# Loading and normalising the first tile of k and q in chunks ahead of the rest of k, with GpSimd normalising the rest

## The chip, the cores and the metric

The kernel runs on one core of a Trainium2 chip. The core has five engines with a queue each, which go through their instructions in order and wait for each other by semaphores: TensorE (PE in the profile; its weight loads are PEld), VectorE (DVE), ScalarE (ACT), GpSimd (POOL) and SyncE (SP, here a queue that issues loads and stores). The metric is the device time of one execution in microseconds (us).

## The reference

```python
def _attn_ref(q, k, v, g_q, g_k):                 # q, k, v: (8, 12, 448, 64) float32
    def rmsnorm(x, g):
        return x / np.sqrt(np.mean(x * x, axis=-1, keepdims=True) + 1e-06) * g
    q_n, k_n = (rmsnorm(q, g_q), rmsnorm(k, g_k))
    scores = 1.0 / np.sqrt(64) * np.matmul(q_n, k_n.transpose(0, 1, 3, 2))
    attn = np.exp(scores - np.max(scores, axis=-1, keepdims=True))
    attn = attn / (np.sum(attn, axis=-1, keepdims=True) + 1e-09)
    return np.matmul(attn, v)
...
x = attn_out.transpose(0, 2, 1, 3).reshape(8 * 448, 12 * 64)
h = x @ w_in                                      # (768, 2048)
return np.maximum(0.01 * h, h) @ w_out            # (2048, 768)
```

So: attention with normalised q and k, and behind it a layer of two matrices with a leaky ReLU between them.

## The kernel before, in words

The attention is cut into 24 units (`u`, three for each of the 8 batches) of four heads. In SBUF a unit's q and k lie as tiles `rq` and `rk` of 128 partitions, with 2 halves (`a`) of 7 groups of rows (`t`) of 64 elements each. One unit goes through these steps:

- `load(u)` issues the loads of q and k on SP's queue. Three buffers of each are in turn, so that the loads of units 1 and 2 could start at once. `hold` puts a small copy on POOL in the way, which writes one element of unit 1's tiles and reads one of a tile of unit 0: the loads of unit 1 wait for that copy, and so for the data that it reads.
- `prep_sq` (ACT) or `prep_sqp` (POOL) squares, `prep_ssq` sums each row's squares on VectorE, `prep_rinv` turns the sums into 1/sqrt on ACT with a Ln and an Exp, `prep_norm` multiplies the row by it on VectorE and writes it as float16 to `n16`.
- The normalised tiles are transposed, in the first units by TensorE (`tr`, `prep_tr`; the bank is then copied to `qkT` by `vcopy` on VectorE or `acopy` on ACT). For q the copy multiplies by the gains: `gcol` is a column that holds 0.125 times g_q times g_k. It is made from two loaded rows: `gdup` (VectorE, line 869) and a small float32 matmul (line 870) that turns the row into a column in the bank `gps`, which is copied to `gcol`.
- `qk` makes the scores of k's tile `t` against all of q in a pair of PSUM banks. For a unit's first tile `shift_max`, `shift_mm` find a maximum over the scores (VectorE, a matmul, VectorE), from which the exponent's shift `eb` is made. `ex` takes the exponential of a score pair on ACT into `et`.
- `zsum`, `pv` sum and weigh with v on TensorE, and later steps divide. Three units make a batch, and then the two matrices follow (`moe1`, lines 432 and 440, then lines 478 and 542).

K0 is k's first tile (0 to 1), K1 the other six (1 to 7); CA and CB are the groups 0 to 4 and 4 to 7.

The order of the work in the opening is written out by hand, line by line, for all engines (lines 858 to 1075); from unit 3 on a plan in a loop mixes attention with the matrices. `warm(n, bank)` is `n` matmuls of a constant that nothing reads (line 847), which keep TensorE running. `gate(u)` is a small copy on POOL that reads the normalised k: what stands behind it in POOL's queue (loads of v and of the weights, squares) waits until VectorE has normalised unit u. In the opening before, q and k of unit 0 are loaded by one transfer each, both on SP; the squares of both stand on ACT, all normalising on VectorE, and the small matmul of the gains stands between 32 and 48 filling matmuls. The lines that decide on the order:

```python
warm(32, wbank)
...                        # gdup, and the matmul of the gains
warm(48, wbank)
prep_sq(0, CA, (0,))
prep_sq(0, CB, (0,))
prep_sq(0, ALL, (1,))
...                        # sums, Ln and Exp for q, then for k
prep_norm(0, CA, (0,))
prep_norm(0, CB, (0,))
prep_norm(0, K0, (1,))
prep_norm(0, K1, (1,))
```

Of the kernel before, what the change touches and what calls it, by code (L numbers as in the profile page):

```python
# [8 lines left out]
FP32 = mybir.dt.float32  # L9
FP16 = mybir.dt.float16  # L10
AF = mybir.ActivationFunctionType
ALU = mybir.AluOpType
AXL = mybir.AxisListType
# [5 lines left out]
def kernel(  # L19
# [11 lines left out]
    nc = tc.nc  # L31

    B, H, S, D = q.shape
    QH = 4
    NS = 7
    P = 128
# [9 lines left out]
    raws = ctx.enter_context(tc.tile_pool(name="raws", bufs=3))  # L46
    prep_p = ctx.enter_context(tc.tile_pool(name="prep", bufs=2))
    small = ctx.enter_context(tc.tile_pool(name="small", bufs=2))
# [12 lines left out]
    def mine(i):  # L61
        return shared or i < 4
# [7 lines left out]
    def aux(bank=None):  # L70
        can = [i for i in free if mine(i) and bank in (None, i)]
        if shared:
            can = [i for i in can[:-1] if i ^ 1 not in free] or can
        free.remove(can[0])
        return single[can[0]]

    def slot():
        if shared:
            can = [i for i in free if i ^ 1 in free]
            last = {i // 2: n for n, i in enumerate(free) if i in can}  # L80
        else:
            last = {i // 2: n for n, i in enumerate(free) if i >= 4 and i ^ 1 in free}
        x = min(last, key=lambda i: last[i])
        for i in (2 * x, 2 * x + 1):
            free.remove(i)
        return double[x]

    def drop(tile_):
        for i in range(8):
            if tile_ is single[i]:  # L90
                assert i not in free
                free.append(i)
                return
        x = [i for i in range(4) if tile_ is double[i]][0]
        assert 2 * x not in free and 2 * x + 1 not in free
        free.extend((2 * x, 2 * x + 1))
# [11 lines left out]
    eps_t = cst.tile([P, 1], FP32)  # L108
# [6 lines left out]
    gcol = cst.tile([P, 1], FP32)  # L115
# [22 lines left out]
    raw = {}  # L138
    st = {}

    def rows(x, u):
        b, g = divmod(u, NQ)
        return x[b, QH * g:QH * g + QH].rearrange("(a r) (p t) d -> (r p) a (t d)", r=2, t=NS)

    def load(u, engines=None, hold=None):
        raw[u] = [raws.tile([P, 2, NS, D], FP32, tag=name, name=name) for name in ("rq", "rk")]
        st[u] = {}
        if hold is not None:
            for t in raw[u]:
                nc.gpsimd.tensor_copy(t[:, 1, NS - 1, D - 1:D], hold[:, 1, NS - 1, D - 1:D])  # L150
        for t, src, eng in zip(raw[u], (q, k), engines or (nc.sync, nc.sync)):
            eng.dma_start(t.rearrange("p a t d -> p a (t d)"), rows(src, u))

    def load_v(u):
        nc.gpsimd.dma_start(vts[u % NV].rearrange("p a t d -> p a (t d)"), rows(v, u))

    ALL = (0, NS)
# [4 lines left out]
        rinv=([P, 2, 2, NS], FP32, 2),  # L162
        n16=([P, 2, NS, 2, D], FP16, 1), qkT=([P, 2, NS, P], FP16, 3))

    def buf(u, name):
        if name not in st[u]:
            shape, dtype, bufs = SHAPES[name]
            st[u][name] = prep_p.tile(shape, dtype, tag=name[:2] if bufs == 3 and name != "qkT" else name, bufs=bufs, name=name)
        return st[u][name]

    BOTH = (0, 1)

    def prep_sq(u, c=ALL, tis=BOTH):
        for ti in tis:
            nc.scalar.activation(buf(u, f"sq{ti}")[:, :, c[0]:c[1]], raw[u][ti][:, :, c[0]:c[1]], AF.Square)  # L175

    def prep_sqp(u, tis=BOTH):
        for ti in tis:
            nc.gpsimd.tensor_tensor(buf(u, f"sq{ti}"), raw[u][ti], raw[u][ti], op=ALU.mult)
# [4 lines left out]
    def prep_ssq(u, c=ALL, tis=BOTH):  # L184
        for ti in tis:
            nc.vector.tensor_reduce(buf(u, "ssq")[:, ti, :, c[0]:c[1]], buf(u, f"sq{ti}")[:, :, c[0]:c[1]],  # L186
                                    axis=AXL.X, op=ALU.add)

    def prep_rinv(u, tis=BOTH):
        x = slice(tis[0], tis[-1] + 1)  # L190
        nc.scalar.activation(buf(u, "uu")[:, x], buf(u, "ssq")[:, x], AF.Ln, bias=eps_t, scale=1.0 / D)
        nc.scalar.activation(buf(u, "rinv")[:, x], buf(u, "uu")[:, x], AF.Exp, bias=0.0, scale=-0.5)  # L192

    def prep_norm(u, c=ALL, tis=BOTH):
        n = c[1] - c[0]
        for ti in tis:
            src = raw[u][ti]
            nc.vector.tensor_tensor(  # L198
                buf(u, "n16")[:, ti, c[0]:c[1]].rearrange("p s a d -> p a s d"), src[:, :, c[0]:c[1]],
                buf(u, "rinv")[:, ti, :, c[0]:c[1], None].broadcast_to([P, 2, n, D]), op=ALU.mult)  # L200

    def as_tp(bank):
        return bank.bitcast(FP16)[:, 0:NS * P].rearrange("p (t x) -> p t x", t=NS)
# [21 lines left out]
    def score(u, t, banks):  # L225
        for r in range(2):
            for a in range(2):
                nc.tensor.matmul(banks[a][64 * r:64 * r + 64, 0:S].rearrange("p (t x) -> p t x", t=NS),  # L228
                                 kT(u, r, a, t), qT(u, r, a), start=True, stop=True)

    def qk(u, steps):
        st[u]["sT"] = []
        for t in steps:
            sT = slot()
            score(u, t, (sT[:, 0], sT[:, 1]))
            st[u]["sT"].append((t, sT))

    def ex(u, most=NS):
        s = st[u]
        if "et" not in s:  # L240
            s["et"] = epool.tile([P, NS, 2, S], FP16, tag="et", name="et")
        for t, sT in s["sT"][:most]:
            nc.scalar.activation(s["et"][:, t], sT[:, :, 0:S], AF.Exp, bias=s["eb"], scale=1.0)  # L243
            drop(sT)
        s["sT"] = s["sT"][most:]
# [15 lines left out]
    def shift_bank(u):  # L261
        st[u]["pb"] = aux()
# [26 lines left out]
    def gate(u):  # L289
        nc.gpsimd.tensor_copy(gate_t, buf(u, "n16")[:, 1, NS - 1, 1, D - 1:D])  # L290
# [550 lines left out]
    CA, CB = (0, 4), (4, NS)  # L841
    K0, K1 = (0, 1), (1, NS)
    VV = ((ALL, vcopy),)

    def warm(n, bank):
        for x in range(n):
            nc.tensor.matmul(bank[:, P:2 * P], onesp, onesp, start=True, stop=True)
# [8 lines left out]
            nc.tensor.matmul(bank[:, S:S + 64], onesp, onesp[:, 0:64], start=True, stop=True)  # L856

    with tc.manual_schedule():
        nc.scalar.dma_start(grow[:, 0], g_q[None, :])
        nc.scalar.dma_start(grow[:, 1], g_k[None, :])  # L860
        nc.scalar.preload_act_table_set("natural_log_exp_and_others")
        load(0)
        load(1, hold=raw[0][1])
        load(2)
        gps = aux()
        wbank = aux()
        warm(32, wbank)
        for a in range(2):
            nc.vector.scalar_tensor_tensor(gdup[:, a], grow[:, 0], 0.125, grow[:, 1], op0=ALU.mult, op1=ALU.mult)
        nc.tensor.matmul(gps[:, 0:1], gdup.rearrange("o a d -> o (a d)"), one32, start=True, stop=True)  # L870
        warm(48, wbank)
        prep_sq(0, CA, (0,))
        prep_sq(0, CB, (0,))
        prep_sq(0, ALL, (1,))
        prep_ssq(0, CA, (0,))
        prep_ssq(0, CB, (0,))
        prep_rinv(0, (0,))
        nc.vector.tensor_copy(gcol, gps[:, 0:1])
        drop(gps)
        prep_ssq(0, ALL, (1,))  # L880
        prep_rinv(0, (1,))
        prep_norm(0, CA, (0,))
        prep_norm(0, CB, (0,))
        prep_norm(0, K0, (1,))
        prep_norm(0, K1, (1,))

        def tr(u, ti, chunks, tp=None, bank=None):
            if tp is None:
                tp = aux(bank)
            for c, copy in chunks:  # L890
                for x in range(*c):
                    nc.tensor.transpose(as_tp(tp)[:, x, :], buf(u, "n16")[:, ti, x].rearrange("p a d -> p (a d)"), ident16)
                copy(buf(u, "qkT")[:, ti, c[0]:c[1]], as_tp(tp)[:, c[0]:c[1]], ti == 0)
            return tp
# [3 lines left out]
        tpk = tr(0, 1, ((K0, vcopy),))  # L898
        warm(6, wbank)
        drop(wbank)  # L900
        prep_sq(1, ALL, (0,))
        qk(0, STEPS[0])
        shift_max(0)
        drop(tr(0, 1, ((K1, acopy),), tpk))
        prep_sq(1, ALL, (1,))
        load(3)
        gate(0)
        load_v(0)
        prep_sqp(2, (0,))
        load_v(1)  # L910
        load_v(2)
        load_w_in(0, 1024)
        shift_bank(0)
        warm(18, st[0]["pb"])
        shift_mm(0)
        drop(st[0]["pb"])
        prep_ssq(1)

        def moe1_third(bank, k0, k1):
            for kt in range(k0, k1):  # L920
# [8 lines left out]
            pv(u, t0, t1)  # L929

        ex(0)
        prep_rinv(1, (0,))
        qk(0, (1,))
        ex(0)
        prep_rinv(1, (1,))
        prep_norm(1, ALL, (0,))
        prep_norm(1, K0, (1,))
        prep_norm(1, K1, (1,))
        load(4)
# [1 line left out]
        prep_sqp(2, (1,))  # L941
        prep_sqp(3, (0,))
        load_w_in(1024, 1024)
        wb = aux()
        warm(20, wb)
        qk(0, (2,))
        ex(0)
        warm(14, wb)
        drop(wb)
        qk(0, (3,))  # L950
# [2 lines left out]
        tpk = tr(1, 1, ((K0, vcopy),), bank=3)  # L953
# [12 lines left out]
        wb = aux(3)  # L966
# [28 lines left out]
        tpk = tr(2, 1, ((K0, vcopy),), bank=1)  # L995
# [81 lines left out]
        for u in range(3, NU):  # L1077
            for d in range(4):
# [103 lines left out]
                if st[u]["sT"]:  # L1182
                    n = 1 if d == 1 and u % 6 == 2 else 0
# [8 lines left out]
        for i, more in enumerate((((xmul, NU - 1, (1,)), (x_sum, B - 1, 3), (x_sum, B - 1, 1)), ((x_sum, B - 1, 2), (x_sum, B - 1, 4)))):  # L1192
            c, fn = queue[i]
# [33 lines left out]
```

## Time and profile before

| | |
|---|---|
| median of 3 runs | 406.6 us (406.59, 406.6, 407.03) |
| the profiled execution | 407.07 us, of which the span of the profile is 405.0 |
| PE, PEld busy | 395.5 us (98%), 223.8 us (55%) |
| DVE, ACT, POOL busy | 317.1 us (78%), 303.6 us (75%), 67.9 us (17%) |
| DMA | 62.87 MB, mean 155 GB/s |

All durations in the text are of the one profiled execution; the median of the runs is 0.47 us below it. A busy share is a mean over the whole span. What the opening is worth is read from the opening: from the start and idle time of its instructions, and from what ended each wait. In a row of the timeline the columns are start, busy time of the group, engine, line, operation, result and source tiles, shapes and the number of instructions; in brackets stands how long the engine sat idle before it and what released it. A few rows of the opening: the first Square on ACT starts at 4.07 us, when q has landed (3.3 us after its issue); the first scores start on PE at 9.62; the first exponential starts on ACT at 12.45.

### The profile page before, as it was taken

To read this page: it belongs to the slowest core of one execution; us is meant where nothing else is said; L and a number is where in the kernel's file an instruction comes from. 1 tells how busy PE (TensorE), PEld (TensorE's weight loads), DVE (VectorE), ACT (ScalarE), POOL (GpSimd) and SP (SyncE) were. 2 spreads that over 40 slices of the span, in tenths; PEclk is the share of its full clock that TensorE was granted. 3 is DMA by queue.
4 is the path that set the end of the run, shared out by engine and by line. 5 is a ranking of instruction groups with operands and counts; after the bars stand their busy time and mean duration, and the time that the engine had idled before them with its cause. 6 is when DMAs were issued, how large, how long until landed. Compare 5 with 4: busy or idle time off the path is not lost.

```text
span 405.0 us, 9412 instructions
## 1 busy us (share of the span) xinstructions
PE 395.5 (98%) x3808; PEld 223.8 (55%) x3808; DVE 317.1 (78%) x501; ACT 303.6 (75%) x474; POOL 67.9 (17%) x86
## 2 busy tenths in 40 slices
PE   8999999999999999999999999999999999999995
PEld 7665454555455544555455544554455557659863
DVE  5888899998879866887779866877679899567672
ACT  5998977789977699778978699868987667744600
POOL 1887431201131201000021200000002200000000
PEclk9999999999999999999999999999999999999999
DMA  6999999989366887579565885678553470122023
GB/s 202 268 243 251 238 236 246 250 205 226 92 160 115 239 213 113 142 195 180 152 159 87 249 230 85 169 164 182 153 100 60 117 164 2 30 56 79 2 68 90
DMA packets 72527, 62.87 MB, mean 155 GB/s; under 512 B 36388, under 2 KB 67620, under 8 KB 72484
## 3 DMA queue, kind: packets, MB, share of 16 engines
q1 hardware_dynamic: 61888, 50.08, 47.2%
q0 software_dynamic: 10272, 11.80, 19.0%
q8 instruction: 30, 0.49, 0.5%
q10 hardware_dynamic: 324, 0.39, 0.3%
q14 instruction: 13, 0.11, 0.1%
HBM read 45.61 MB, written 11.01 MB: 140 GB/s over the span
## 4 chain that ended last, share of the span: by engine, by line
PE 81%; DVE 4%; DMA 3%; issue 1%; SPq 1%; ACT 1%; DVEq 0%
PE banks L432 26%; PE banks L542 23%; PE banks L228 8%; PE banks L478 8%; PE banks L678 6%; PE banks L410 6%; DMA rz<-zs 3%; PE banks L347 2%; DVE banks L257 1%; PE banks L276 1%; DVE n L198 1%; SPq L378 1%; DVE ost L549 1%; PE banks L440 1%; PE banks L210 0%
## 5 line engine op out<-in xcount | busy, mean ns | idle before, releaser
L243 ACT ACTIVATE et<-banks,eb 128x896 f16<-128x896 f32 x168 | 160.5, 1008 | 22.9 <-PE banks L228 22.1
L432 PE MATMUL banks<-xt,win 128*128 128x448 f16 x606 | 121.1, 353 | 0.0
L432 PEld LDWEIGHTS <-win 128*128 128x128 f16 x606 | 57.0, 98 | 55.8 <-issue 7.0
L426 ACT ACTIVATE gt<-banks 128x448 f16<-128x448 f32 x104 | 55.2, 551 | 8.3 <-PE banks L432 6.6
L228 PE MATMUL banks<-qkT 64*64 64x448 f16 x672 | 49.6, 361 | 1.6 <-DVE qkT L833 0.8
L186 DVE TENSOR_REDUCE ssq<-sq 128x14 f32<-128x896 f32 (+2 forms) x49 | 50.3, 1058 | 0.7 <-ACT sq L175 0.7
L542 PEld LDWEIGHTS <-sa 128*128 128x128 f16 x352 | 33.5, 98 | 25.0 <-issue 3.9
L542 PE MATMUL banks<-tw,sa 128*128 128x384 f16 x264 | 46.9, 326 | 0.0
L549 DVE TENSOR_TENSOR ost<-banks,ost 128x384 f32<-128x384 f32 x55 | 30.4, 553 | 13.3 <-PE banks L542 12.6
L410 PE MATMUL banks<-et,vt 64*64 64x448 f16 x672 | 36.9, 349 | 0.0
L542 PEld LDWEIGHTS <-gt 128*128 128x128 f16 x264 | 25.5, 98 | 18.2 <-issue 1.7
L478 PE MATMUL banks<-wout,gt 128*128 128x384 f16 x192 | 33.7, 326 | 0.0
L293 POOL COPY gate_t<-qkT 128x1 f16<-128x1 f16 x16 | 4.9, 304 | 169.0 <-DMA qkT<-n 169.0
L228 PEld LDWEIGHTS <-qkT 64*64 64x64 f16 x672 | 16.8, 105 | 29.5 <-issue 22.3
L542 PE MATMUL banks<-wout,gt 128*128 128x384 f16 x176 | 32.4, 326 | 0.0
L198 DVE TENSOR_TENSOR n<-rq,rinv 128x896 f16<-128x896 f32 (+2 forms) x25 | 30.3, 1215 | 1.9 <-ACT rinv L192 1.9
L257 DVE TENSOR_REDUCE banks<-banks 128x1 f32<-128x896 f32 x24 | 26.3, 1096 | 6.0 <-PE banks L228 4.7
L331 DVE TENSOR_TENSOR ea<-ea,et 128x896 f16<-128x896 f16 x36 | 22.5, 624 | 8.0 <-ACT et L243 6.9
L198 DVE TENSOR_TENSOR n<-rk,rinv 128x896 f16<-128x896 f32 (+2 forms) x26 | 28.0, 1084 | 0.0
L331 DVE TENSOR_TENSOR ea<-et 128x896 f16<-128x896 f16 x20 | 13.2, 658 | 17.1 <-ACT et L243 17.1
L410 PEld LDWEIGHTS <-vt 64*64 64x64 f16 x672 | 20.0, 107 | 10.0
L478 PEld LDWEIGHTS <-gt 128*128 128x128 f16 x192 | 18.0, 98 | 13.7 <-issue 2.9
(111 smaller groups left out, 488.1 us busy)
## 6 DMA issues: line engine op xcount, KB each, us to landing
rq<-in_q_dram SPq DMA_DIRECT2D x24, 448.0 KB, 5.6
rk<-in_k_dram SPq DMA_DIRECT2D x24, 448.0 KB, 6.5
out_dram<-ost SPq DMA_DIRECT2D x52, 192.0 KB, 3.3
rz<-zs SPq DMA_DIRECT2D x80, 112.0 KB, 4.1
vt<-in_v_dram POOLq DMA_DIRECT2D x24, 224.0 KB, 5.6
win<-in_moe_w_in_dram POOLq DMA_DIRECT2D x8, 384.0 KB, 15.7
wout<-in_moe_w_out_dram POOLq DMA_DIRECT2D x2, 1536.0 KB, 29.1
out_dram<-ost SPq DMA_DIRECT2D x4, 96.0 KB, 2.2
```

The source lines that it names most:

```text
L186: nc.vector.tensor_reduce(buf(u, "ssq")[:, ti, :, c[0]:c[1]], buf(u, f"sq{ti}")[:, :, c[0]:c[1]], axis=AXL.X, op=ALU.add)
L198: nc.vector.tensor_tensor(buf(u, "n16")[:, ti, c[0]:c[1]].rearrange("p s a d -> p a s d"), src[:, :, c[0]:c[1]], buf(u, "rinv")[:, ti, :, ...
L228: nc.tensor.matmul(banks[a][64 * r:64 * r + 64, 0:S].rearrange("p (t x) -> p t x", t=NS), kT(u, r, a, t), qT(u, r, a), start=True, stop=True)
L243: nc.scalar.activation(s["et"][:, t], sT[:, :, 0:S], AF.Exp, bias=s["eb"], scale=1.0)
L257: nc.vector.tensor_reduce(s["spare"][:, 511:512], sT[:, :, 0:S], axis=AXL.XY, op=ALU.max)
L331: nc.vector.tensor_tensor(s["ea"], s["et"][:, 0] if t == 1 else s["ea"], s["et"][:, t], op=ALU.add)
L410: nc.tensor.matmul(s["pv"][r][64 * a:64 * a + 64, 0:S], vts[u % NV][64 * r:64 * r + 64, a, t], s["et"][64 * r:64 * r + 64, t, a], start=(t ...
L426: nc.scalar.activation(dst, src, AF.Prelu, bias=0.0, scale=1.0, alpha=0.01)
L432: nc.tensor.matmul(hps[:, 0:S], win16[:, kt // 2, kt % 2, ts(ft, P)], xt[:, kt // 2, kt % 2], start=(kt == 0), stop=(kt == KT - 1))
L478: nc.tensor.matmul(op2[:, 0:HC], gt[:, ft, ds(col(t), P)], wout16[:, ft, ds(HC * half, HC)], start=(i == 0), stop=(i == FT - 1))
L542: nc.tensor.matmul(bank[:, 0:HC], a[:, f], b[:, f], start=(first and f == 0), stop=(f == HF - 1), skip_group_check=not first)
L549: nc.vector.tensor_tensor(dst, g[name][:, 0:HC], src, op=ALU.add)
```

## The change

The change writes the opening anew. Loads: k's first tile comes alone, on ACT's queue; q in two chunks and then the rest of k on SP. The hold of unit 1's loads reads q's first chunk instead of the end of k. k's first tile and q are squared, summed and put through one common Ln and Exp (`first_q`, `first_r`); the rest of k follows with its own. The matmul of the gains stands behind all 80 filling matmuls, and its copy to `gcol` goes from VectorE to ACT, ahead of the square of the rest of k. The rest of k is normalised by POOL in two parts, tiles 1 and 2 (KA) and 3 to 6 (KB), which are transposed and copied separately, KA by ACT, KB by VectorE. The square of unit 1's q goes from ACT to POOL. `gate(0)` is gone. Unit 1's Ln and Exp stand one exponential later, its sum of k behind the copy of KB, and some filling matmuls are moved or added (22 for 18).

```diff
-                nc.gpsimd.tensor_copy(t[:, 1, NS - 1, D - 1:D], hold[:, 1, NS - 1, D - 1:D])
+                nc.gpsimd.tensor_copy(t[:, 1, NS - 1, D - 1:D], hold)
...
-    def prep_norm(u, c=ALL, tis=BOTH):
+    def prep_norm(u, c=ALL, tis=BOTH, rinv=None, eng=nc.vector):
...
+        KA, KB = (1, 3), (3, NS)
+        first_q = small.tile([P, 2, NS + 1], FP32, tag="first_q", bufs=1, name="first_q")
+        first_r = small.tile([P, 2, NS + 1], FP32, tag="first_r", bufs=1, name="first_r")
...
+        load_part(nc.scalar, 1, K0)
+        load_part(nc.sync, 0, CA)
+        load_part(nc.sync, 0, CB)
+        load_part(nc.sync, 1, K1)
         nc.scalar.dma_start(grow[:, 0], g_q[None, :])
         nc.scalar.dma_start(grow[:, 1], g_k[None, :])
         nc.scalar.preload_act_table_set("natural_log_exp_and_others")
-        load(0)
-        load(1, hold=raw[0][1])
+        load(1, hold=raw[0][0][:, 1, 3, D - 1:D])
         load(2)
         gps = aux()
         wbank = aux()
         warm(32, wbank)
+        warm(48, wbank)
+        prep_sq(0, K0, (1,))
+        prep_sq(0, CA, (0,))
+        prep_sq(0, CB, (0,))
+        for ti, c, o in ((1, K0, NS), (0, CA, 0), (0, CB, 4)):
+            nc.vector.tensor_reduce(first_q[:, :, o:o + c[1] - c[0]], buf(0, f"sq{ti}")[:, :, c[0]:c[1]], axis=AXL.X, op=ALU.add)
+        nc.scalar.activation(first_q, first_q, AF.Ln, bias=eps_t, scale=1.0 / D)
+        nc.scalar.activation(first_r, first_q, AF.Exp, bias=0.0, scale=-0.5)
         for a in range(2):
             nc.vector.scalar_tensor_tensor(gdup[:, a], grow[:, 0], 0.125, grow[:, 1], op0=ALU.mult, op1=ALU.mult)
         nc.tensor.matmul(gps[:, 0:1], gdup.rearrange("o a d -> o (a d)"), one32, start=True, stop=True)
-        warm(48, wbank)
-        prep_sq(0, CA, (0,))
-        prep_sq(0, CB, (0,))
-        prep_sq(0, ALL, (1,))
-        prep_ssq(0, CA, (0,))
-        prep_ssq(0, CB, (0,))
-        prep_rinv(0, (0,))
-        nc.vector.tensor_copy(gcol, gps[:, 0:1])
+        nc.scalar.copy(gcol, gps[:, 0:1])
+        prep_sq(0, K1, (1,))
+        prep_norm(0, CA, (0,), first_r[:, :, 0:4])
+        prep_norm(0, CB, (0,), first_r[:, :, 4:NS])
+        prep_norm(0, K0, (1,), first_r[:, :, NS:NS + 1])
         drop(gps)
-        prep_ssq(0, ALL, (1,))
-        prep_rinv(0, (1,))
-        prep_norm(0, CA, (0,))
-        prep_norm(0, CB, (0,))
-        prep_norm(0, K0, (1,))
-        prep_norm(0, K1, (1,))
...
         tpk = tr(0, 1, ((K0, vcopy),))
         warm(6, wbank)
         drop(wbank)
-        prep_sq(1, ALL, (0,))
+        prep_ssq(0, K1, (1,))
+        prep_sqp(1, (0,))
+        x = buf(0, "uu")[:, 1, :, 1:NS]
+        nc.scalar.activation(x, buf(0, "ssq")[:, 1, :, 1:NS], AF.Ln, bias=eps_t, scale=1.0 / D)
+        nc.scalar.activation(buf(0, "rinv")[:, 1, :, 1:NS], x, AF.Exp, bias=0.0, scale=-0.5)
         qk(0, STEPS[0])
         shift_max(0)
-        drop(tr(0, 1, ((K1, acopy),), tpk))
+        prep_norm(0, KA, (1,), None, nc.gpsimd)
+        prep_norm(0, KB, (1,), None, nc.gpsimd)
         prep_sq(1, ALL, (1,))
         load(3)
-        gate(0)
         load_v(0)
         prep_sqp(2, (0,))
...
-        warm(18, st[0]["pb"])
+        warm(22, st[0]["pb"])
         shift_mm(0)
         drop(st[0]["pb"])
-        prep_ssq(1)
+        tr(0, 1, ((KA, acopy),), tpk)
+        prep_ssq(1, ALL, (0,))
...
         ex(0)
+        qk(0, (1,))
+        drop(tr(0, 1, ((KB, vcopy),), tpk))
+        prep_ssq(1, ALL, (1,))
+        ex(0)
         prep_rinv(1, (0,))
-        qk(0, (1,))
+        prep_norm(1, ALL, (0,))
+        wb = aux()
+        warm(20, wb)
+        qk(0, (2,))
         ex(0)
         prep_rinv(1, (1,))
-        prep_norm(1, ALL, (0,))
         prep_norm(1, K0, (1,))
         prep_norm(1, K1, (1,))
         load(4)
         gate(1)
         prep_sqp(2, (1,))
         prep_sqp(3, (0,))
         load_w_in(1024, 1024)
-        wb = aux()
-        warm(20, wb)
-        qk(0, (2,))
-        ex(0)
         warm(14, wb)
```

More of the change, by code (lines that the diff above doesn't have):

```diff
@@ L197, in prep_norm @@
             src = raw[u][ti]
-            nc.vector.tensor_tensor(
+            r = buf(u, "rinv")[:, ti, :, c[0]:c[1], None] if rinv is None else rinv[:, :, :, None]
+            eng.tensor_tensor(
                 buf(u, "n16")[:, ti, c[0]:c[1]].rearrange("p s a d -> p a s d"), src[:, :, c[0]:c[1]],
-                buf(u, "rinv")[:, ti, :, c[0]:c[1], None].broadcast_to([P, 2, n, D]), op=ALU.mult)
+                r.broadcast_to([P, 2, n, D]), op=ALU.mult)
     def as_tp(bank):
@@ L858, with load_part @@
     with tc.manual_schedule():
+        KA, KB = (1, 3), (3, NS)
+        first_q = small.tile([P, 2, NS + 1], FP32, tag="first_q", bufs=1, name="first_q")
+        first_r = small.tile([P, 2, NS + 1], FP32, tag="first_r", bufs=1, name="first_r")
+        raw[0] = [raws.tile([P, 2, NS, D], FP32, tag=name, name=name) for name in ("rq", "rk")]
+        st[0] = {}
+        def load_part(eng, ti, c):
+            eng.dma_start(raw[0][ti][:, :, c[0]:c[1]].rearrange("p a t d -> p a (t d)"),
+                          rows((q, k)[ti], 0)[:, :, D * c[0]:D * c[1]])
+        load_part(nc.scalar, 1, K0)
+        load_part(nc.sync, 0, CA)
+        load_part(nc.sync, 0, CB)
+        load_part(nc.sync, 1, K1)
         nc.scalar.dma_start(grow[:, 0], g_q[None, :])
```

## The prediction

> **What bounds the kernel now.** The page first, then the chain of waits, then the timeline of each engine over the opening, where the change acts. The chain, in order of time, begins
>
> ```profile
> 26 pieces in order of time: start us, us, what
> 38.94 0.04 issue
> 38.99 0.38 PE banks L302 x4
> 39.37 0.38 PE banks L410 x8
> 39.75 0.86 PE banks L440 x4
> ```
>
> and from there to 405 it is nearly all TensorE (PE 81% of the span). So an opening that reaches 38.9 later by x ends the kernel later by x, unless something between absorbs it. The opening on ScalarE:
>
> ```profile
> 8.38 1.16 ACT L837 ACTIVATE qkT<-banks,gcol 128x512 f16<-128x512 f16 x2 [0.51 <-PE banks L892]
> 9.43 0.95 ACT L175 ACTIVATE sq<-rq 128x896 f32<-128x896 f32 x1
> 10.48 0.80 ACT L839 COPY qkT<-banks 128x768 f16<-128x768 f16 x1
> 11.18 0.95 ACT L175 ACTIVATE sq<-rk 128x896 f32<-128x896 f32 x1
> 12.45 1.01 ACT L243 ACTIVATE et<-banks,eb 128x896 f16<-128x896 f32 x1 [0.32 <-DVE eb L287]
> ...
> 18.50 3.72 ACT L243 ACTIVATE et<-banks,eb 128x896 f16<-128x896 f32 x4 [0.47 <-PE banks L228]
> ```
>
> The first exponential waits for the shift (DVE eb), 2.83 us after the first score (PE, 9.62). At 18.50 ACT waits again: the scores it needs stand on PE behind unit 1's first score, which hangs on VectorE. VectorE has no pause from 12.33 to 17.25:
>
> ```profile
> 12.33 2.07 DVE L186 TENSOR_REDUCE ssq<-sq 128x14 f32<-128x896 f32 x2
> 14.32 1.08 DVE L198 TENSOR_TENSOR n<-rq,rinv 128x896 f16<-128x896 f32 x1
> 15.36 1.16 DVE L198 TENSOR_TENSOR n<-rk,rinv 128x128 f16<-128x128 f32 x2
> ```
>
> So two things set the time here: when the first score is there, and how long VectorE needs from the first shift to unit 1's normalised k. On TensorE the filling matmuls:
>
> ```profile
> 1.16 3.60 PE L847 MATMUL banks<-onesp 128*128 128x128 f16 x32 [1.16 <-DVE onesp L107]
> 4.68 0.58 PE L870 MATMUL banks<-one,g_t 1*128 1x1 f32 x2
> 5.20 2.91 PE L847 MATMUL banks<-onesp 128*128 128x128 f16 x48
> 7.95 0.90 PE L892 MATMUL banks<-ident,n 128*128 128x128 f16 x8
> ```
>
> 32 of them take 3.60 us (107 ns from start to start in the trace), 48 take 2.91 (56 ns, after two slower ones at 5.2 to 5.4). The matmul of the gains stands between.
>
> **Loads.** q and k of unit 0 land at 4.05 and 5.20 now. 192 KB less ahead of the first chunk, at the 0.39 MB/us of the steady part, is 0.5 us, but k's first tile (64 KB, beside it on ACT's queue) takes up to 0.2 back: q's first chunk lands near 3.7 to 3.9, the second near 4.4, the rest of k near 5.4. 256-byte rows by the hundred are not in the trace; between their bytes (0.2 us) and the price of as many 1,792-byte rows (1.2 us) I take 0.2, nearest by size. ACT's queue gains an issue of some 0.5 us (SP's took 0.46) ahead of the gains' loads and the table load (1.28), which then ends near 3.3, still before the data. SP has three issues instead of two, done by 2.2.
>
> **Opening up to the transposes: earlier.** Squares on ACT: 128 elements about 0.3 (512 took 0.63, 384 took 0.51), then 0.63 and 0.51, done near 5.0; three reductions on VectorE done near 5.8 (before, 5.89 for q alone); Ln and Exp (0.30, 0.21) to 6.35. Now VectorE starts the normalising at 6.4 instead of 7.21, since k's full reduction (1.09) and a second Ln and Exp are gone from the front. k's first tile is done near 7.8 instead of 8.57: 0.8 us gained, if it were what the score waits for.
>
> **The first score: later.** It also needs the gains. Their matmul now stands behind all 80 filling matmuls. TensorE starts at 1.16; at 107 ns, 39 of them run up to 5.35, where the trace's pace changes, and 41 more at 56 ns end at 7.65. The gains' matmul (0.58 for two passes at the slow pace, half that at best; I take 0.5) ends at 8.15. ACT copies the column at 8.2 (short ACT rows 0.21), and behind that copy, in ACT's queue, stands the square of the rest of k: 768 elements between 0.63 and 0.95, so 0.85, started at 8.3. Only then, at 9.05, come the two scaled copies of q (1.16 together), to 10.2; first score 10.25 against 9.62: **0.65 later**. What the copy holds up is all of that; the transposes were ready near 7.5 to 8.6. The first exponential comes at 13.1.
>
> **What is taken off does not count.** VectorE's normalising of the rest of k (0.95, 8.48 to 9.43) lay before a wait of 0.49 for PE. ACT's square of unit 1's q (0.95) and the shorter copy of k (256 for 768 elements, about 0.4 less) lay at 9.43 to 12.13, ahead of a wait for eb. Of k's sum, 768 of 896 elements move behind the square (9.1 to 10.05), still ahead of the first maximum at 10.7.
>
> **Unit 1's chain: longer.** After eb VectorE now sums q of unit 1 (1.04), then copies k's last four tiles (512 elements, between 0.22 for 128 and 0.55 for 768: 0.40, net 0.35), then sums k. And ACT puts unit 1's Ln and Exp for q behind the second exponential instead of the first, for k behind the third instead of the second (0.9 each). q is normalised from 15.45 (14.32 before: 0.65 + 0.35 + 0.1 of waiting for ACT). k's first tile waits for its Exp: exponentials at 13.1, 14.0, pair to 15.35, third to 16.25, pair to 16.8, so 16.8 against 15.36: **1.4 later**. From there to unit 1's shift nothing changes, so unit 1's first exponential comes at 21.7 instead of 20.31; ACT, which has used up unit 0's scores, waits.
>
> **What hides the rest.** POOL takes the square of unit 1's q (1.68), and two normalisings of 256 and 512 elements; with POOL's sq row (1.68 for 896) to its xt row (128x896 f16, 2.23) as ends, 0.5 to 0.65 and 1.0 to 1.3, I take the upper, the type being f16. From the Exp at 10.75 they end near 11.4 and 12.7. k's tiles 1 and 2 are transposed behind the shift matmul (12.2), copied by ACT at 12.5 in 0.4, just before the exponential: no cost; if POOL took twice as long, 0.3. v of unit 0 leaves POOL at 12.7 instead of 9.61; its first use is at 22.9 and landing takes 7.9 median in this stretch, so over 3 us are spare. The first w_in loads go from 15.2 to about 16.5, used at 39.7. gate(0) goes, 0.19. Unit 1's loads leave SP at 4.3 instead of 5.46, behind the rest of k on the same queue: nothing needs them before 7. The four more filling matmuls (0.22) and the 20 moved ones lie where PE waits for dg and for ACT.
>
> **After 20 us.** ACT runs without a pause from 18.50 to 31.1, VectorE's waits there are for ACT (n <- ACT rinv, 0.64), ACT's pauses at 31.8 (0.71) and 39.4 (0.51) are ended by the same chain. So the 1.4 stays. Sum: 407.07 (profiled execution; span 405.0 and 2.07 around it) + 1.4 = 408.5; the median of the runs lies 0.47 lower, so 406.6 + 1.4 = **408.0**.
>
> The Trainium skill, "TensorE: Matmul & The Clock Gate", section "What you observe", has 128-column matmuls go from about 107 to 56 ns some 4 us into sustained activity, give or take 0.5 us between runs. The trace agrees: 4.19 us after the first. By that rule the change of pace falls between 4.66 and 5.66, and the sum between 1.1 and 1.55.
>
> **Rivals.** (1) *The pace changes much earlier.* Every us by which it comes before 5.35 takes 0.5 us off (107 against 56 ns), so before about 4.1 the loss is under 0.8: 406.6 to 407.4. One execution shows 5.35; nothing ties it to the kernel's start. 0.15.
> (2) *Faster.* The gains are through by 6.3, so that the 0.8 gained by k's first tile reaches the score, and unit 1's Ln and Exp find cover instead of adding: 405.8. It decides if the gains' matmul ends by 6.3, 1.85 us earlier than the rows allow. Against it: 80 matmuls in one queue at never under 56 ns are 4.5 us, 5.6 with the start. 0.08.
> (3) *Absorbed.* The delay is used up in the pauses before 39 us: 406.6, within half a us. For it: ACT pauses of 0.47, 0.71 and 0.51. Against: each ends with PE or VectorE, which are late as well. 0.07.
> (4) *Worse: POOL and VectorE collide.* Unit 1's q can land at 7, and POOL's ungated square then meets VectorE's normalising. Such a meeting is in the trace:
>
> ```profile
> 118.13 1.08 DVE L198 TENSOR_TENSOR n<-rq,rinv 128x896 f16<-128x896 f32 x1
> 119.13 2.97 DVE L198 TENSOR_TENSOR n<-rk,rinv 128x896 f16<-128x896 f32 x1
> ```
>
> and on POOL
>
> ```profile
> 118.16 2.99 POOL L388 TENSOR_TENSOR xt<-x,rz 128x896 f16<-128x896 f32 x1 [0.19 <-DMA rz<-zs]
> ```
>
> 2.97 for a step of 1.08: it stood until POOL ended, 121.15. Behind POOL's 1.68 k's first tile would be done at 9.6, its copy at 10.2, the sum of k at 11.1, the maximum 0.4 later: 408.4, to 409 with slow small rows. 0.08. The Trainium skill's "SBUF — State Buffer", section "Who interferes with whom", has a VectorE instruction with two SBUF inputs and a GpSimd read exclude each other in full; the rows agree.
>
> **Numbers.** My own case, 407.5 to 408.5: 0.62. Faster by over 0.2% (0.8 us, what can be told from no change): rival 2, 0.08. Within: rivals 1 and 3, 0.22. Slower: 0.70. Range 406.7 to 409.0; outside it are rival 2 and the low ends of 1 and 3.
>
> **What would show it.** The gains' matmul near 7.65; ACT's copy of gcol at 8.2, square, q's copies to 10.2; first score 10.25, first exponential 13.1; unit 1's k normalised at 16.8; a wait of ACT near 20.5 to 21.7. I am wrong if the first exponential comes before 12.45, or if unit 1's first comes at 20.3 all the same.

## The result, and the profile after

The changed kernel is **slower**: 408.5 us median of 22 runs (407.62 to 409.7) against 407.29 us of 22 runs of the kernel before (406.32 to 409.3). The ratio is 1.0029, with a 95% interval of 1.0019 to 1.004: some 1.2 us. The profiled execution took 408.63 us, with a span of 406.7; before it was 407.07 with 405.0.

ScalarE's timeline in the opening (start, busy time, instruction; in brackets the idle time before it and what ended it):

```profile
8.39 0.16 ACT L893 COPY gcol<-banks 128x1 f32<-128x1 f32 x1 [1.79 <-PE banks L892]
8.45 0.85 ACT L175 ACTIVATE sq<-rk 128x768 f32<-128x768 f32 x1
9.19 1.15 ACT L838 ACTIVATE qkT<-banks,gcol 128x512 f16<-128x512 f16 x2
...
13.22 1.91 ACT L244 ACTIVATE et<-banks,eb 128x896 f16<-128x896 f32 x2
```

It waits 1.79 us for the small matmul of the gains (line 892), then squares the rest of k, and only then makes the two scaled copies of q. The first exponential comes at 13.22 (12.45 before). The wait ahead of the stretch in which unit 1's exponentials begin has grown from 0.47 to 1.18 us, and the stretch starts at 20.06 instead of 18.50:

```profile
20.06 3.72 ACT L244 ACTIVATE et<-banks,eb 128x896 f16<-128x896 f32 x4 [1.18 <-PE banks L229]
```

The same opening on TensorE:

```profile
1.16 6.88 PE L848 MATMUL banks<-onesp 128*128 128x128 f16 x80 [1.16 <-DVE onesp L107]
7.97 0.38 PE L892 MATMUL banks<-one,g_t 1*128 1x1 f32 x2
8.29 0.62 PE L905 MATMUL banks<-ident,n 128*128 128x128 f16 x8
...
10.39 0.38 PE L229 MATMUL banks<-qkT 64*64 64x448 f16 x4 [1.15 <-ACT qkT L838]
```

The last line is the first score; it waits for ScalarE's copies of q. In the kernel before it waited for VectorE's copy of k's first tile:

```profile
9.62 0.38 PE L228 MATMUL banks<-qkT 64*64 64x448 f16 x4 [0.44 <-DVE qkT L833]
```

The changed kernel on VectorE:

```profile
7.71 0.28 DVE L199 TENSOR_TENSOR n<-rk,first_r 128x128 f16<-128x128 f32 x1
...
13.10 1.07 DVE L186 TENSOR_REDUCE ssq<-sq 128x14 f32<-128x896 f32 x1
14.09 0.41 DVE L834 COPY qkT<-banks 128x512 f16<-128x512 f16 x1
14.42 1.07 DVE L186 TENSOR_REDUCE ssq<-sq 128x14 f32<-128x896 f32 x1
15.65 1.09 DVE L199 TENSOR_TENSOR n<-rq,rinv 128x896 f16<-128x896 f32 x1 [0.15 <-issue]
16.93 1.16 DVE L199 TENSOR_TENSOR n<-rk,rinv 128x128 f16<-128x128 f32 x2 [0.19 <-ACT rinv L192]
```

Two losses are to be read here. First, k's first tile is normalised by 7.99 (8.57 before), yet the first score stands at 10.39 (9.62 before): all 80 filling matmuls stand in TensorE's queue ahead of the gains' matmul, and ahead of the transposes as well. Second, from the end of the first shift (13.1) VectorE now does a sum, a copy, a sum and two normalisings with two short waits, and unit 1's k starts at 16.93 (15.36 before). The chain of waits from 30 us on is the one of before, 1.62 us later (40.56 for 38.94):

```profile
40.56 0.04 issue
40.60 0.38 PE banks L303 x4
```

The account can be made with two points of ScalarE's timeline, the first exponential (A) and the start of the stretch with the wait ahead of unit 1's exponentials (B): A is 0.77 us later, and B minus A has grown from 6.05 to 6.84, by 0.79. Together they are 1.56. Of A's 0.77, about 0.28 (an estimate) is not the change's: in this execution the filling matmuls went over to their fast pace 0.56 us later than in the one before (5.91 for 5.35, see the table below), and each us of that costs about half a us ahead of A. Without it the two losses are about 1.3 us, near the 1.2 between the medians.

That the span is 1.7 longer is in part chance. The chain's groups of matmuls stay about 1.6 us late up to 248.62 (247.06 before). Then the chains of the two profiles take different ways: a transfer, `rz<-zs`, is on the chain of the kernel before twice,

```profile
266.60 4.00 DMA rz<-zs
281.57 6.80 DMA rz<-zs
```

and on that of the changed kernel once:

```profile
268.17 3.52 DMA rz<-zs
```

Behind them the delay is 0.96 (295.38 for 294.42), and it is 0.98 at the last long group of matmuls (383.39 for 382.41); another 0.7 comes after that group. Why the two executions part there is not shown; the change is in the opening alone. So the span of one execution says less than A, B and the medians.

### The profile page after: what moved, and what is told of

Read it like the earlier page. It is cut to its first block, busy times and chain, and to the rows that moved or that the text cites. A ratio compares the mean times of both kernels' runs of the same rounds, so it can differ in the third digit from the quotient of the medians.

```text
span 406.7 us, 9427 instructions
## 1 busy us (share of the span) xinstructions
PE 395.5 (97%) x3812; PEld 224.2 (55%) x3812; DVE 316.4 (78%) x501; ACT 302.6 (74%) x475; POOL 69.6 (17%) x88
## 4 chain that ended last, share of the span: by engine, by line
PE 85%; DVE 2%; DMA 1%; issue 1%; SPq 0%; ACT 0%; DVEq 0%
PE banks L433 29%; PE banks L543 23%; PE banks L229 9%; PE banks L479 8%; PE banks L411 6%; PE banks L679 6%; PE banks L348 2%; DMA rz<-zs 1%; PE banks L277 1%; PE banks L441 1%; DVE banks L258 1%; DVE ost L550 1%; SPq L379 0%; PE banks L211 0%; PE banks L939 0%
## 5 line engine op out<-in xcount | busy, mean ns | idle before, releaser
L186 DVE TENSOR_REDUCE ssq<-sq 128x14 f32<-128x896 f32 (+1 forms) x47 | 49.1, 1073 | 0.2 <-ACT sq L175 0.2
L294 POOL COPY gate_t<-qkT 128x1 f16<-128x1 f16 x16 | 3.9, 243 | 169.6 <-DMA qkT<-n 169.6
L199 DVE TENSOR_TENSOR n<-rq,rinv 128x896 f16<-128x896 f32 x23 | 30.8, 1339 | 2.1 <-ACT rinv L192 2.0
L199 DVE TENSOR_TENSOR n<-rk,rinv 128x896 f16<-128x896 f32 (+2 forms) x24 | 25.0, 1044 | 0.2 <-ACT rinv L192 0.2
```

The lines of the kernel that those rows point to most:

```text
L199: eng.tensor_tensor(buf(u, "n16")[:, ti, c[0]:c[1]].rearrange("p s a d -> p a s d"), src[:, :, c[0]:c[1]], r.broadcast_to([P, 2, n, D]), o ...
```

## The experiments

**My theory:** half of the loss is the place of the gains' matmul behind all the filling matmuls (it sets A), half is the new order of unit 1's steps (it sets B minus A). **Rivals:** the loss comes from ScalarE's square of the rest of k in front of q's copies; from the earlier loads of unit 1; or from GpSimd's part. The pace of the filling matmuls is a matter of its own: the time at which it goes from 107 to 56 ns from start to start differs between executions, from 3.93 to 7.00 us in the eleven profiles. So the table has it beside A and B. (It shows in the starts of the matmuls: in the profile after, 12 or 13 a us from 3 to 6 us and 22 from 6 to 7, while the granted clock reads 1.00 in both stretches.)

| kernel | median us (runs) | ratio to before, 95% | change of pace | first score | A | B | B minus A |
|---|---|---|---|---|---|---|---|
| before | 407.29 (22) | | 5.35 | 9.62 | 12.45 | 18.50 | 6.05 |
| changed | 408.5 (22) | 1.0029 (1.0019 to 1.004) | 5.91 | 10.39 | 13.22 | 20.06 | 6.84 |
| d1_fewer | 407.64 (12) | 1.0001 (0.9986 to 1.0016) | 6.60 | 9.27 | 12.09 | 18.93 | 6.84 |
| d2_more | 410.52 (6) | 1.0076 (1.006 to 1.0092) | 5.25 | 12.32 | 15.14 | 21.99 | 6.85 |
| d3_rinv | 408.2 (12) | 1.0014 (1.0001 to 1.0026) | 6.55 | 10.70 | 13.52 | 19.84 | 6.32 |
| d4_both | 406.98 (12) | 0.9989 (0.998 to 0.9999) | 4.70 | 9.35 | 12.73 | 19.05 | 6.32 |
| d5_filled | 407.17 (12) | 0.9994 (0.9978 to 1.0011) | 5.58 | 9.20 | 12.02 | 18.36 | 6.34 |
| d6_square | 408.93 (12) | 1.0035 (1.0018 to 1.0051) | 6.20 | 10.13 | 14.03 | 20.87 | 6.84 |
| d7_dve | 409.68 (10) | 1.0046 (1.0023 to 1.0069) | 4.21 | 9.59 | 12.88 | 19.73 | 6.85 |
| d8_hold | 407.36 (12) | 1.0 (0.9984 to 1.0017) | 7.00 | 10.36 | 13.18 | 19.23 | 6.05 |
| d9_gains | 408.51 (12) | 1.0031 (1.0009 to 1.0052) | 3.93 | 9.68 | 12.51 | 19.35 | 6.84 |

The last column is the plainest finding: it takes three values only. 6.05 is the old order, 6.84 the changed one, 6.32 to 6.34 the changed one with unit 1's Ln and Exp put back. It doesn't depend on anything that happens before A. (The runs of d7_dve were on another chip, where the kernel before had a median of 407.65; in the others it had 407.29 to 407.42.)

**d1_fewer: 52 filling matmuls ahead of the gains' matmul instead of 80.**

```diff
-        warm(48, wbank)
+        warm(20, wbank)
```

> The changed kernel with 20 instead of 48 filling matmuls in the second group, nothing else: 28 x 56 ns = 1.57 us less ahead of the gains' matmul (7.97 in the changed kernel). Theory A (the first score waits for that matmul, then ACT's copy and square): gains' matmul near 6.4, first score near 9.0 (10.39 before this edit), bounded then by k's first tile and the square; first exponential near 12.1 instead of 13.22, where it meets the next wait, the copy of k's tiles 1 and 2, which hang on GpSimd. Unit 1's first exponential (21.9 in the changed kernel) 0.6 to 0.9 earlier, the span 0.6 to 0.9 shorter. Theory B (unit 1's longer chain on VectorE sets the time, the first score has cover): first score earlier, but span within 0.2 of 406.7. Theory C (loads and GpSimd set the opening): first exponential stays near 13.2.

ScalarE:

```profile
7.16 0.16 ACT L893 COPY gcol<-banks 128x1 f32<-128x1 f32 x1 [0.38 <-PE banks L892]
...
12.09 1.91 ACT L244 ACTIVATE et<-banks,eb 128x896 f16<-128x896 f32 x2
```

Measured: the gains' column is copied at 7.16 instead of 8.39, the first exponential comes 1.13 us earlier although the change of pace came 0.7 later in this execution, and the median falls by 0.86 us, to that of the kernel before. The first loss is thus the length of the queue ahead of the gains' matmul and the transposes. The rest of the changed order is as it was, and its wait of 1.18 us stands. The twelve runs lie in two groups, six of 407.0 to 407.5 and six of 407.8 to 408.3; d4_both below shows what goes with the second.

**d2_more: 120 filling matmuls ahead of it.**

```diff
-        warm(48, wbank)
+        warm(88, wbank)
```

> The changed kernel with 88 instead of 48 filling matmuls in the second group: 40 x 56 ns = 2.24 us more ahead of the gains' matmul. Theory A: gains' matmul at 10.2, first score at 12.6, first exponential at 15.4, unit 1's first exponential and the span all 2.2 later (408.9). Theories B and C: the span grows by clearly less than 2.2, since another wait covers part.

ScalarE:

```profile
10.31 0.16 ACT L893 COPY gcol<-banks 128x1 f32<-128x1 f32 x1 [3.48 <-PE banks L892]
...
15.14 1.91 ACT L244 ACTIVATE et<-banks,eb 128x896 f16<-128x896 f32 x2
```

40 more matmuls at 56 ns are 2.24 us; the first exponential came 1.92 later, which is the 2.24 less 0.33 for a change of pace 0.66 earlier (half as much, since a matmul at 107 ns is as long as two at 56). The median rose by 2.0 us. So between medians a us on TensorE ahead of the gains' matmul is a us at the end of the kernel: the delay is not absorbed.

**d3_rinv: unit 1's Ln and Exp one exponential earlier again, and its sum of k ahead of the copy of KB.**

```diff
         ex(0)
+        prep_rinv(1, (0,))
+        prep_ssq(1, ALL, (1,))
         qk(0, (1,))
         drop(tr(0, 1, ((KB, vcopy),), tpk))
-        prep_ssq(1, ALL, (1,))
         ex(0)
-        prep_rinv(1, (0,))
+        prep_rinv(1, (1,))
         prep_norm(1, ALL, (0,))
...
         ex(0)
-        prep_rinv(1, (1,))
```

> The changed kernel with unit 1's Ln and Exp back one exponential earlier on ACT (behind the first and the second), and the copy of k's last four tiles behind the sum of unit 1's k on VectorE. The first score and first exponential stay at 10.4 and 13.2. Theory A, whose second part is unit 1's chain (1.4 in all, 0.65 of it from the score): unit 1's k normalised 0.55 earlier (16.4 instead of 16.93), unit 1's first exponential and the span 0.5 to 0.55 shorter. If the front alone set the time, nothing moves; if the chain's length comes from GpSimd's normalising, nothing moves either.

VectorE:

```profile
13.41 2.07 DVE L186 TENSOR_REDUCE ssq<-sq 128x14 f32<-128x896 f32 x2
15.39 0.41 DVE L834 COPY qkT<-banks 128x512 f16<-128x512 f16 x1
15.72 1.08 DVE L199 TENSOR_TENSOR n<-rq,rinv 128x896 f16<-128x896 f32 x1
16.72 1.15 DVE L199 TENSOR_TENSOR n<-rk,rinv 128x128 f16<-128x128 f32 x2
```

The two short waits ahead of the normalisings are gone, and B minus A is 0.52 us shorter. Its profile also has a change of pace 0.64 later, which takes 0.3 back; the median fell by 0.3 us, with intervals that overlap, so it is the trace and not the time that shows this gain. The 0.27 us by which 6.32 is above the old 6.05 are about as long as the copy of KB, which is new in this place: 0.33 from its start to the next instruction's (15.39 to 15.72). So of the second loss, 0.79, some 0.5 are unit 1's Ln and Exp and the place of its sum, which this run does not tell apart; that the rest is the copy is worked out from this row and not tested.

**d4_both and d5_filled: the edits of d1_fewer and d3_rinv together, in d5_filled with twelve of the filling matmuls put behind the gains' matmul.** Beside the edits shown, d5_filled has

```diff
         nc.scalar.copy(gcol, gps[:, 0:1])
+        warm(12, wbank)
```

> The edits of the two runs together (20 filling matmuls; unit 1's Ln and Exp one exponential earlier). If the two parts simply add, the span is 1.1 to 1.4 shorter than the changed kernel's 406.7. From the rows of the changed kernel I expect less: with the score at 9.0 GpSimd's square of unit 1's q (9.23 to 10.9, behind its landing) stands ahead of the normalising of k's tiles, so the copies of those tiles bound the first two exponentials; unit 1's first exponential near 20.9, as in the run with fewer matmuls alone, the span 0.6 to 1.0 shorter.

> The run with 20 filling matmuls and unit 1's Ln and Exp earlier, with 12 more filling matmuls behind the gains' matmul, where TensorE stood idle from 6.96 to 7.64 in that run and then ran at the slow pace from 8.1 to 11.5. If that slow stretch cost it the gain (its shift came 0.6 late), TensorE stays at the full pace, first score near 9.2, first exponential near 12.05 instead of 12.73, unit 1's first exponential near 20.4 instead of 20.85, span near 404.5. If the slow stretch is chance, as the first change of pace is (4.70 to 6.60 in the runs so far), it shows here too and the span stays near 405.2.

Both losses are taken back: 406.98 and 407.17 us, against 407.42 and 407.39 of the kernel before, measured beside each. The gain was expected to fall short of the sum of the parts (0.6 to 1.0 us); d4_both is 1.5 us below the changed kernel, where the medians of d1_fewer and d3_rinv add to 1.16. The opening of d5_filled reaches A 0.43 us before the old kernel (12.02), loses 0.29 of that up to B (18.36), and ends with the same span, 405.0, where 404.5 was expected. What the rest of the change gains is small at most: the interval of d4_both's ratio ends at 0.9999, that of d5_filled's includes 1.

The profile of d4_both shows something else, in its windows of 1 us (window, its length, then busy time and number of instructions of PE, PEld, DVE, ACT and POOL, the granted clock, the DMA share, GB/s):

```profile
6.00:7.00 1.00, 0.38 (x2) 0.29 (x2) 0.63 (x4) 0.53 (x3) 0.00 (x0) 1.00 0.89 299
7.00:8.00 1.00, 0.36 (x4) 0.22 (x4) 1.00 (x3) 0.90 (x2) 0.00 (x0) 1.00 0.99 360
8.00:9.00 1.00, 0.93 (x10) 0.90 (x10) 0.50 (x4) 0.86 (x2) 0.25 (x1) 0.56 1.02 321
9.00:10.00 1.00, 1.00 (x10) 0.42 (x8) 0.85 (x2) 0.43 (x2) 1.00 (x1) 0.50 1.00 326
10.00:11.00 1.00, 1.00 (x11) 1.00 (x11) 1.00 (x1) 0.97 (x3) 0.93 (x2) 0.50 1.00 375
11.00:12.00 1.00, 1.00 (x17) 1.00 (x14) 0.37 (x2) 0.26 (x1) 1.00 (x2) 0.74 1.02 391
```

After two us in which TensorE was busy for less than 0.4 of the time, the granted clock falls to 0.50 for 3.41 us (8.12 to 11.53). The filling matmuls ahead of the shift's small matmul then take longer, and the first exponential comes at 12.73, against 12.02 in d5_filled. The same 22 matmuls in d4_both and in d5_filled:

```profile
9.87 2.17 PE L848 MATMUL banks<-onesp 128*128 128x128 f16 x22
```

```profile
9.52 1.40 PE L848 MATMUL banks<-onesp 128*128 128x128 f16 x22
```

d5_filled, with its 12 matmuls at 6.74 us, has no such stretch in its profile, and none of its twelve runs has a mean granted clock below 0.997. Two of d4_both's have (0.994, 0.995), and six of d1_fewer's (0.993 to 0.995), whose spans are 406.0 to 406.3 us against 405.1 to 405.6 for its other six. In the medians of d4_both and d5_filled the difference doesn't show, and that the twelve matmuls prevent the fall is not shown: ten of d4_both's twelve runs have a mean of 0.997 or more without them.

**d6_square: ScalarE's square of the rest of k behind q's copies.** The rival that ScalarE's queue is the cause:

```diff
         nc.scalar.copy(gcol, gps[:, 0:1])
-        prep_sq(0, K1, (1,))
...
         tpk = tr(0, 1, ((K0, vcopy),))
...
+        prep_sq(0, K1, (1,))
         prep_ssq(0, K1, (1,))
```

> The changed kernel with ACT's square of the rest of k moved behind the two scaled copies of q. Theory A as first put (the square holds up the copies, 0.75 of the delay): first score 0.75 earlier, 9.65. But the sum of that square stands on VectorE ahead of the first maximum, so it ends near 11.2 instead of 10.3 and the maximum starts then instead of at 10.82, and GpSimd's normalising of k is late by as much: first exponential near 13.8 instead of 13.2, span 0.3 to 0.6 longer than 406.7. If the score alone decided, the span would be 0.7 shorter.

VectorE:

```profile
10.85 0.95 DVE L186 TENSOR_REDUCE ssq<-sq 128x12 f32<-128x768 f32 x1 [1.54 <-ACT sq L175]
11.71 1.09 DVE L258 TENSOR_REDUCE banks<-banks 128x1 f32<-128x896 f32 x1
```

The score comes only 0.26 us earlier (10.13), not 0.75, because q's transposes stand behind the gains' matmul too and end just after it. (The change of pace is 0.29 later here; at the same pace it would be some 0.4, an estimate.) And the sum of the rest of k, which stands ahead of the first maximum on VectorE, now waits 1.54 us for the late square: the maximum starts at 11.71 instead of 10.82, the first exponential 0.81 later than in the changed kernel. The median is 0.4 us above the changed kernel's, and the intervals overlap; there is no gain. So the square is a part of the way on which the late gains reach the score, some 0.4 of the 0.77; it is not the loss's cause by itself, and putting it behind q's copies does not take that part back.

**d7_dve: the rest of k normalised by VectorE instead of GpSimd.**

```diff
-        prep_norm(0, KA, (1,), None, nc.gpsimd)
-        prep_norm(0, KB, (1,), None, nc.gpsimd)
+        prep_norm(0, KA, (1,))
+        prep_norm(0, KB, (1,))
```

> The changed kernel with the two normalisings of the rest of k of unit 0 (tiles 1 and 2, tiles 3 to 6) on VectorE instead of GpSimd, at the same place in the order, between the step behind the first maximum and the one that makes the shift. Theory (VectorE is the engine that carries the opening, so GpSimd's share is a gain of its own that the later gains' matmul and the later Ln and Exp outweigh): VectorE needs about 0.35 + 0.6 us for them, of which some 0.4 lies in its wait for the small matmul; the first exponential comes 0.5 to 1.5 us after the changed kernel's, unit 1's first pair about 1 later, the span longer by 0.5 to 1.5: about 409.5 median, ratio to the kernel before about 1.005. Rival (GpSimd's share is worth nothing, since VectorE had an idle stretch for it as in the kernel before): within 0.3 us of the changed kernel, 408.2 to 408.8.

VectorE:

```profile
11.22 0.29 DVE L260 TENSOR_TENSOR dg<-ident,banks 128x128 f16<-128x128 f16 x1
11.42 1.02 DVE L199 TENSOR_TENSOR n<-rk,rinv 128x256 f16<-128x256 f32 x2
12.36 0.30 DVE L284 TENSOR_REDUCE banks<-banks 128x1 f32<-128x128 f32 x1
```

From the first score to the first exponential it is 3.29 us instead of 2.83: 0.46 more, just under the theory's low end, since part of the 1.02 lies in the wait of 0.38 for the shift's matmul. So in this profile GpSimd's part is worth about half a us. The times do not settle it: against the kernel before the median is 2.0 us higher, where the changed kernel's is 1.2 higher, but the ten runs lie in two groups (four of 407.3 to 408.2, six of 409.7 to 410.4), the profile is of the lower one, and that one is no slower than the changed kernel. Five of the upper six have a mean granted clock of 0.995 or 0.996, the lower four 0.997 to 1.000; what else makes up the upper group, this run does not show.

**d8_hold: the kernel before, with only the hold of the changed kernel.** The rival that the earlier loads of unit 1 do harm:

```diff
-                nc.gpsimd.tensor_copy(t[:, 1, NS - 1, D - 1:D], hold[:, 1, NS - 1, D - 1:D])
+                nc.gpsimd.tensor_copy(t[:, 1, NS - 1, D - 1:D], hold)
...
-        load(1, hold=raw[0][1])
+        load(1, hold=raw[0][0][:, 1, 3, D - 1:D])
```

> The kernel before, with one part of the change: unit 1's loads wait for the end of unit 0's q instead of the end of its k. Nothing in the opening waits for unit 1's loads before 9.4 and they landed at 9.03. All theories but one: loads issued near 4.25 instead of 5.46, time unchanged within 0.2%. If the load order was worth something in itself, or if k of unit 0 is slowed by the traffic beside it, the first exponential moves from 12.45.

No difference: 407.36 against 407.39 us. Its profile happens to be of an execution with a late change of pace, and shows that the kernel before hangs on it as well. TensorE:

```profile
5.20 3.69 PE L847 MATMUL banks<-onesp 128*128 128x128 f16 x48
8.73 0.61 PE L892 MATMUL banks<-ident,n 128*128 128x128 f16 x8
```

The 48 matmuls took 3.69 instead of 2.91 us, the transposes stood at 8.73 instead of 7.95, the first exponential at 13.18 instead of 12.45, and B is 0.73 later as well. (Unit 0's k landed at 5.47 instead of 5.20 in this profile, but the score waited for q's copies.) The span is 406.3 instead of 405.0; of that 1.3 the pace is 0.7, and the rest came after 250 us, where this chain too takes a way of its own. So the sums above are best made from A, B and the medians.

**d9_gains: the gains' row and matmul back between the 32 and the 48.**

```diff
         warm(32, wbank)
+        for a in range(2):
+            ...                     # gdup
+        nc.tensor.matmul(gps[:, 0:1], gdup.rearrange("o a d -> o (a d)"), one32, start=True, stop=True)
         warm(48, wbank)
...                                  # and taken out behind the common Ln and Exp
```

> The changed kernel with the gains' row (VectorE) and matmul back between the 32 and the 48 filling matmuls, all 80 of them kept. Theory A (the first score waits for that matmul, then ACT's copy and square): both leave the path, ACT's square starts near 6.8, the score waits for the 80 filling matmuls and q's transposes and copies alone: 9.6 to 10.0 by when the pace changes, instead of 10.39; first exponential 12.4 to 12.7, span 0.4 to 0.7 shorter than 406.7. If the square and the gains had no part in it, the score stays at 10.4.

TensorE:

```profile
4.99 0.38 PE L884 MATMUL banks<-one,g_t 1*128 1x1 f32 x2 [0.56 <-DVE g_t L883]
5.29 2.85 PE L848 MATMUL banks<-onesp 128*128 128x128 f16 x48
7.99 0.61 PE L905 MATMUL banks<-ident,n 128*128 128x128 f16 x8
```

In the median there is no gain: 408.51 us, the changed kernel's time. TensorE waited 0.56 us for the gains' row, whose loads now stand behind k's first tile on ScalarE's queue, and the transposes still stand behind all 80 filling matmuls, at 7.99 against 8.29, in the execution with the earliest change of pace of all (3.93). In this profile the score (9.68) and the first exponential (12.51) came where they were expected, and A and B are both 0.71 earlier than in the changed kernel; the span is only 0.2 shorter, where 0.4 to 0.7 was expected, and five of the twelve runs took 409.0 to 410.8 us. So by the times, moving the small matmul alone isn't enough, while d1_fewer, with 28 fewer matmuls in front of the transposes and the gains together, is. How much of the loss is the gains' place by itself, this run leaves open.

**Not tried:** taking the copy of KB off VectorE, and a lower number of filling matmuls in the old order.

## Why the prediction was right, point by point

The direction, the size and both mechanisms held: 408.0 us with a loss of 1.4 were forecast, and 408.5 with a loss of 1.2 between medians (1.56 at B between the profiles) were measured. The half us between 408.0 and 408.5 is the base, which ran at 407.29 over 22 runs and not at the 406.6 of the three runs shown: 0.69 more, less the 0.2 by which the loss was smaller. That the profile's 1.56 is so near to 1.4 is partly luck, since 0.28 of it is a later change of pace.

- *Opening up to the transposes, k's first tile done near 7.8:* 7.99, 0.58 earlier than before instead of 0.8. That it isn't what the score waits for held.
- *First score later by 0.65:* 0.77. The steps came in the order forecast: gains' matmul 7.97 (forecast 7.65), copy 8.39 (8.2), q's copies from 9.19 to 10.3 (10.2), score 10.39 (10.25). The term that was too small is the filling matmuls: the change of pace came at 5.91 instead of 5.35, and 0.56 times a half is 0.28 of the 0.32 by which the gains' matmul was later. That matmul took 0.38, not 0.5. The Trainium skill, "TensorE: Matmul & The Clock Gate", section "What's actually happening", says that the first window of some 3.4 us that is busy throughout releases the clock, and that the windows run freely, so that the cold count differs from run to run. By that the change would fall 3.4 to 6.8 us after the first matmul (an estimate from that page); the eleven profiles have 2.8 to 5.8, so the spread agrees and the lower end does not: in d9_gains TensorE was busy for 2.77 of the 3.41 us before the change. The 0.5 us either way that the prediction took from "What you observe" was too narrow for these executions.
- *"What the copy holds up is all of that; the transposes were ready near 7.5 to 8.6":* wrong in its reason. The transposes stand behind the gains' matmul in the same queue and ran from 8.29. d6_square shows what this means: with the square out of the way q's copies start only 0.27 earlier (8.92 for 9.19).
- *Unit 1's chain 1.4 later:* k's first tile at 16.93 (16.8), 1.57 later than before, which is 0.77 from the score and 0.79 from the order. d3_rinv takes 0.52 of the second part away by the Ln and Exp and the place of the sum, and leaves 0.27; the prediction had 0.35 for the copy and about 0.4 for the waits.
- *A wait of ACT near 20.5 to 21.7:* it stands earlier, from 18.88 to 20.06, in the place of the old wait of 0.47. Unit 1's first exponential, two further on, comes 1.56 later than before, at 21.87 (21.7 forecast).
- *After 20 us the loss stays whole:* so it does up to 250 us (1.62 at 40.6), and d2_more gives 2.0 us at the end for 1.92 at A. That single executions part again behind 250 us (0.6 back in this one, and 0.7 lost again at the end) the prediction did not have.
- *What is hidden:* held, with two sizes off. GpSimd's two normalisings took 1.62 us together, nearer to the lower bound (1.5) than to the upper (1.95) that was taken; the rest of k landed at 6.05, not 5.4; neither lay on the path. Unit 1's q landed at 9.1, not at 7, so GpSimd's square never met VectorE's normalising: rival 4 did not arise.
- *Rival 1, an earlier change of pace,* is real as a mechanism (3.93 and 4.21 occurred), but moves the kernel before as well, as d8_hold shows from the other side. *Rivals 2 and 3* fell: a copy of gcol as early as 6.84 (d5_filled) or 6.73 (d9_gains) needs fewer filling matmuls ahead of the gains than the change has, and the pauses before 39 us absorb nothing.

## What to carry to other kernels

In a queue that runs in order, a small instruction that others wait for goes behind no more filling work than its own data takes to come; filling that is there to keep TensorE running belongs behind it, in the waits. A step saved ahead of a wait is worth nothing until what ends that wait is early too: here the normalised k was 0.58 us earlier and the score 0.77 later. And when work is moved off the busiest engine, look at what was moved past what in the other queues: putting unit 1's Ln and Exp one exponential later, and its sum behind a copy, cost 0.52 us, as much as GpSimd's help brought in the one profile that shows it (0.46).

## What was not expected of the hardware

- The time at which 128-column matmuls go from 107 to 56 ns lay between 3.93 and 7.00 us after the start in eleven profiles, though TensorE began at 1.16 in each. The kernel before and its copy with another hold differ by 0.73 us at A and B with it.
- The clock was halved again for 3.41 us after two us in which TensorE was busy for less than 40% of the time, not idle (d4_both); 12 more matmuls in that stretch went with a profile without it (d5_filled).
- The first load of 64 KB in rows of 256 bytes, alone on ScalarE's queue, landed at 3.98 us, after the 256 KB of q's first chunk on SP's (3.78); and the second row of gains, some 0.2 KB, landed at 4.42.
